# A speech joint network, forward and backward: GpSimd's sum of the tanh gradient over prompts, one instruction of 1024 columns or two of 512

## The chip, the core and the metric

The kernel runs on one core of a Trainium2 chip. The metric is the device time of one execution in microseconds (us); the time of a kernel is the median of its runs. The core has five engines with a queue of instructions each: TensorE (PE in the profile, its weight loads PEld), VectorE (DVE), ScalarE (ACT), GpSimd (POOL) and SyncE (SP), which here only issues DMAs. An engine works through its queue in order, and waits at an instruction until the semaphores it needs have been raised by others.

## The reference

All tensors are bfloat16. `x` has 2 x 16000 x 256 elements, the prompts `g` 2 x 8 x 256; `B`, `U`, `D` are 2, 8 and 256.

```python
h = gelu(conv(x, w1))[:, ::2]        # 3 taps, 256 -> 256, every second time step is kept
f = gelu(conv(h, w2))[:, ::2]        # the same again: 4000 steps per batch entry
fe = f @ w_f;  ge = g @ w_g
j  = tanh(fe[:, :, None, :] + ge[:, None, :, :])     # 4000 x 8 prompts x 256
out = j @ w_o
```

The kernel returns `out` and the gradients of all seven inputs for a given `grad_out` of the shape of `out`. For the gradient of `fe`, the gradient at the input of the tanh, `(grad_out @ w_o.T) * (1 - j*j)`, is summed over the eight prompts. That sum is what the change touches.

## The kernel before

The 4000 steps of each batch entry are cut into chunks of 512 (the last has 416), 16 chunks in all. Features lie on the 128 partitions, so that 256 features are two halves `kt` (0 and 1) side by side in a tile `[128, 2, 512]`.

The main loop (line 763) goes over the chunks `n`. For each it goes through four pairs of prompts. `joint_units` (603) is the main stream: for each prompt `u` of the pair `gj` (519) computes the tanh gradient, then comes the addition of `ngfe_acc` (537), and then the output product (line 624) and the gradient of `w_o` (line 673). `weave` (682) feeds two other things between the steps of this stream. The one is a list of units on TensorE: the two convolutions and the `w_f` product of chunk `n+1` (lines 244, 280, 303), and the backward pass of chunk `n-1` (lines 337, 367, 381 to 383, 407, 438, 479, 501). The other is `later`, a queue of single instructions of the two GELUs and their derivatives, of which `pump(2)` takes two at each step. They are all recorded at line 194 and run on VectorE, except for a sigmoid on ScalarE. So the order of each engine's queue follows from this weaving, and instructions of different parts stand close together.

The instructions that the prediction's steps touch:

- `gj`, line 532: for each half `mt`, VectorE reads the product of line 530 out of PSUM, multiplies it by `j*j - 1` (`JSQ`, squared by ScalarE at line 524) and writes one half of `NGZ`, the negated tanh gradient of this prompt. There are three buffers of `NGZ`. With the result VectorE also writes a sum over the columns, in a short instruction of its own after it (DVE_READ_ACCUMULATOR).
- `ngfe_acc`, line 551: GpSimd adds `NGZ` of prompts 0 and 1 into `ACCN` (float32), then one prompt after the other, and writes the sum with prompt 7 to `NGFE` (bfloat16): seven additions in a chunk, each over `[128, 1024]`. There is one buffer of `ACCN` and one of `NGFE`.
- Line 194 on VectorE: in the first part of a GELU `g_sq<-g_x` (a square, TENSOR_TENSOR), `g_sq<-g_sq` (a multiplication by a number, TENSOR_SCALAR), `g_s<-g_sq,g_x` (SCALAR_TENSOR_TENSOR), ScalarE's sigmoid, and `HT<-g_s,g_x`; in the second, `g_sq<-g_sq`, `g_x<-g_s`, `g_sq<-g_sq,g_x`, `g_sq<-g_sq,HT` and `G<-g_sq,g_s`. All their operands lie in SBUF.
- Lines 339, 370, 383, 323: VectorE's reads of the backward pass's products out of PSUM (`GF`, `GH`, `rows`, `ACC`).
- GpSimd's queue holds, besides the additions, the issues of the stores of `out` (line 653) and of the gradient of `x` (line 491), of the loads of `x` for the backward pass (line 180), and small copies of one or two columns at chunk borders (lines 235, 259, 263, 331, 343, 358, 374).

TensorE's products go through a ring of seven PSUM buffers (`psp`, line 96). A product can start when the engine that reads the product before it in the same buffer has done so.

Of the kernel before, what the change touches and what calls it, by code (L numbers as in the profile page):

```python
# [15 lines left out]
ALU = mybir.AluOpType  # L16
# [6 lines left out]
KT = 2  # L23
# [3 lines left out]
U = 8  # L27
# [4 lines left out]
def kernel(  # L32
# [22 lines left out]
    nc = tc.nc  # L55
# [7 lines left out]
    def geom(n):  # L63
        b, ci = chunks[n]
        c0 = ci * CW
        return b, ci, c0, min(CW, MQ - c0)
# [470 lines left out]
    def ngfe_acc(n, u):  # L537

        W = geom(n)[3]
        st = S[n]  # L540
        if u == 0:
            return
        if u == 1:
            st["ACCN"] = accp.tile([P, KT, CW], FP32, name="ACCN")
        acc = st["ACCN"][:, :, :W]
        in0 = st["NGZ", 0][:, :, :W] if u == 1 else acc
        out = acc
        if u == U - 1:
            st["NGFE"] = ngp.tile([P, KT, CW], BF16, name="NGFE")
            out = st["NGFE"][:, :, :W]  # L550
        nc.gpsimd.tensor_tensor(out=out, in0=in0, in1=st["NGZ", u][:, :, :W], op=ALU.add)  # L551

    def load_jr(n, up):

# [48 lines left out]
    def joint_units(n, up, ahead):  # L603
# [4 lines left out]
        for u in us:  # L608
            yield from gj(n, u)
            ngfe_acc(n, u)  # L610
            short_jt(n, u)
# [280 lines left out]
```

## Time and profile before

| | |
|---|---|
| median of 3 runs | 883.72 us (882.99 to 883.83) |
| the profiled execution's own time | 882.75 us |
| its span, from the first to the last instruction | 881.0 us |
| busy: PE, DVE, ACT, POOL | 833.0, 678.9, 639.0, 419.6 us |
| granted TensorE clock over the span | 0.993 |
| line 551 on POOL, by shape | 98 instructions of 1024 columns, 14 of 832; busy 247.8 us in all (162.7 + 30.2 + 30.2 + 17.7 + 3.5 + 3.5) |
| DVE instructions of line 532 | 256, 680 ns each for 512 columns |

The profile has a page with the busy time of the engines, the chain of work that ended last, and the costliest groups of instructions. The trace behind it can be asked for the order in time of each engine's instructions (the timeline), for who waited for whom, and for the chain in any stretch. A line of the timeline has the start in us, the duration in us, the engine, the line of the kernel, the operation, out<-in with the shape of the tile, how many were merged, and in brackets how long the engine was idle before it and whose instruction ended that.

The work between 120 and 800 us repeats chunk by chunk, every 52.7 us (the same addition starts at 553.47 and at 606.15 us), so one chunk can be read for most of them.

### The profile page before, as it was taken

Reading aid. Unit: us, or ns where it says so; the run is one execution under the profiler, and the core shown is the slowest. Engines: PE = TensorE matmul, PEld = TensorE weight load, DVE = VectorE, ACT = ScalarE, POOL = GpSimd, SP = SyncE. Lnnn points to the kernel's source line nnn. Section 1 sums busy time; section 2 is a strip of 40 time slices with the busy share of each in tenths; the row PEclk is TensorE's granted clock in tenths of the full one; section 3 lists DMA queues with packets and bytes.
Section 4 is the critical chain, followed back from the end, with each engine's and each line's share of the span. In section 5 each row is a group of like instructions: output and inputs, shape, how many; then the busy total and the mean of one; then the engine's idle time right before and its main releaser. Section 6 shows DMA issues by size and latency. Waiting matters only on the chain.

```text
span 881.0 us, 17824 instructions
## 1 busy us (share of the span) xinstructions
PE 833.0 (95%) x6574; PEld 600.6 (68%) x6648; DVE 678.9 (77%) x1296; ACT 639.0 (73%) x1016; POOL 419.6 (48%) x457
## 2 busy tenths in 40 slices
PE   7968999999999999998999999999999999999997
PEld 3545676767768577776756668676776757778875
DVE  5998959869596895959789596986959779596553
ACT  2767797686958769595786958768695876958534
POOL 1254544535535455553554544454554535554651
PEclk9998999999999999999999999999999999999999
DMA  9987999999999999999999999999999999997942
GB/s 207 183 182 164 191 229 233 219 210 231 239 227 229 239 179 258 196 227 214 183 197 201 250 219 224 246 230 250 198 227 225 222 237 194 229 209 175 225 136 94
DMA packets 382456, 185.67 MB, mean 211 GB/s; under 512 B 330160, under 2 KB 366280, under 8 KB 382368
## 3 DMA queue, kind: packets, MB, share of 16 engines
q1 hardware_dynamic: 362400, 114.35, 74.3%
q0 software_dynamic: 19968, 70.18, 26.9%
q8 instruction: 52, 0.85, 0.4%
q14 instruction: 36, 0.29, 0.1%
HBM read 54.43 MB, written 50.34 MB: 119 GB/s over the span
## 4 chain that ended last, share of the span: by engine, by line
PE 42%; DVE 29%; ACT 20%; issue 5%; DMA 2%; POOL 0%; ACTq 0%; POOLq 0%; DVEq 0%
DVE g_sq L194 10%; ACT JT L313 8%; PE GWO_ps L673 6%; PE ps L479 5%; PE ps L501 5%; PE ps L624 5%; DVE g_s L194 4%; PE ps L530 4%; PE ps L438 4%; PE ps L280 4%; PE pst L381 3%; DVE NGZ L532 3%; ACT GX L482 3%; DVE GH L370 3%; ACT JSQ L524 3%
## 5 line engine op out<-in xcount | busy, mean ns | idle before, releaser
L551 POOL TENSOR_TENSOR ACCN<-ACCN,NGZ 128x1024 f32<-128x1024 f32 (+1 forms) x80 | 180.3, 2254 | 174.5 <-DVE NGZ L532 173.3
L532 DVE SCALAR_TENSOR_TENSOR NGZ<-JSQ,ps 128x512 bf16<-128x512 bf16 (+1 forms) x256 | 164.2, 668 | 85.6 <-ACT GX L482 40.6
L524 ACT ACTIVATE JSQ<-JT 128x1024 bf16<-128x1024 bf16 (+1 forms) x128 | 135.3, 1059 | 76.2 <-DVE NGZ L532 76.2
L313 ACT ACTIVATE JT<-FE,GE 128x512 bf16<-128x512 f32 (+1 forms) x256 | 171.2, 738 | 0.1
L624 PE MATMUL ps<-WO,JT 128*128 128x256 bf16 x992 | 147.7, 273 | 5.7 <-DVE NGZ L532 4.9
L626 ACT CAST OUT<-ps 128x512 bf16<-128x512 f32 x248 | 143.4, 605 | 5.1 <-PE ps L624 4.7
L530 PE MATMUL ps<-GOT,WOT 128*128 128x512 bf16 (+1 forms) x472 | 134.2, 373 | 9.4 <-DVE GH L370 7.6
L673 PE MATMUL GWO_ps<-GO,JR 128*128 128x256 bf16 x992 | 139.0, 273 | 0.0
L194 ACT ACTIVATE g_s<-g_s 128x1024 bf16<-128x1024 bf16 (+2 forms) x49 | 49.3, 1005 | 98.0 <-DVE g_s L194 98.0
L624 PEld LDWEIGHTS <-JT 128*128 128x128 bf16 x992 | 94.6, 98 | 31.1 <-issue 9.5
L673 PEld LDWEIGHTS <-JR 128*128 128x128 bf16 x992 | 95.0, 98 | 23.8 <-issue 8.5
L323 DVE TENSOR_TENSOR ACC<-ACC,ps 128x512 f32<-128x512 f32 x90 | 59.2, 680 | 59.9 <-PE ps L501 55.3
L479 PE MATMUL ps<-W1T,GH 128*128 128x256 bf16 (+2 forms) x768 | 104.2, 273 | 0.4 <-ACT g_x L283 0.4
L501 PE MATMUL ps<-rows,X 128*128 128x256 bf16 (+2 forms) x768 | 92.3, 273 | 0.0
L244 PE MATMUL ps<-XC,W 128*128 128x512 bf16 (+1 forms) x370 | 88.6, 374 | 0.7 <-DMA XC<-in_x_dram 0.5
L482 ACT CAST GX<-ps 128x512 bf16<-128x512 f32 (+2 forms) x128 | 76.5, 598 | 14.1 <-PE ps L479 7.4
L479 PEld LDWEIGHTS <-GH 128*128 128x128 bf16 (+2 forms) x768 | 75.0, 99 | 15.9 <-issue 1.8
L501 PEld LDWEIGHTS <-X 128*128 128x128 bf16 (+2 forms) x768 | 74.6, 98 | 12.9 <-issue 1.3
L530 PEld LDWEIGHTS <-WOT 128*128 128x128 bf16 x512 | 49.0, 98 | 48.3 <-issue 9.5
L491 POOL DMA_DIRECT2D out_dram<-GX x64 | 35.7, 558 | 88.8 <-ACT GX L482 84.6
L653 POOL DMA_DIRECT2D out_dram<-OUT x64 | 49.4, 773 | 59.8 <-ACT OUT L626 54.7
L383 ACT COPY rows<-pst 128x1024 bf16<-128x1024 bf16 x64 | 64.2, 1013 | 10.7 <-PE pst L381 10.7
(135 smaller groups left out, 1324.0 us busy)
## 6 DMA issues: line engine op xcount, KB each, us to landing
GO<-in_grad_out_dram SPq DMA_DIRECT2D x56, 512.0 KB, 5.2
out_dram<-OUT POOLq DMA_DIRECT2D x56, 512.0 KB, 5.6
X<-in_x_dram POOLq DMA_DIRECT2D x58, 320.0 KB, 8.0
out_dram<-GX POOLq DMA_DIRECT2D x58, 256.0 KB, 3.8
JR<-JT SPq DMA_TRANSPOSE x240, 4.8
GO<-in_grad_out_dram SPq DMA_DIRECT2D x8, 384.0 KB, 4.0
out_dram<-OUT POOLq DMA_DIRECT2D x8, 384.0 KB, 4.9
GOT<-in_grad_out_dram SPq DMA_TRANSPOSE x128, 5.0
```

Source lines behind the costliest of these rows:

```text
L194: later.popleft()()
L313: nc.scalar.activation(out=JT[:, mt, :W], in_=S[n]["FE"][:, mt, :W], func=ACT.Tanh, bias=GE[:, b, mt, u:u + 1], scale=1.0)
L479: nc.tensor.matmul(ps[:Mx, cj * D:(cj + 1) * D], lhsT=GH[:, par, kt, j:j + Mx], rhs=W1T[:, i, kt, :], start=(k == 0), stop=(k == last))
L482: nc.scalar.copy(out=t[:Mx, 2 * cp:2 * cp + 2, :], in_=ps[:Mx, :])
L501: nc.tensor.matmul(ps[:, dt * D:(dt + 1) * D], lhsT=st["X5", o][:M, i + 2 * par, dt * P:(dt + 1) * P], rhs=t[:M, j + 2 * par:j + 2 * par + ...
L524: nc.scalar.activation(out=JSQ[:, :, :W], in_=JT[:, :, :W], func=ACT.Square)
L530: nc.tensor.matmul(ps[:, :W], lhsT=WOT[:, kt, mt * P:(mt + 1) * P], rhs=GOT[:, kt, :W], start=(kt == 0), stop=(kt == KT - 1))
L532: nc.vector.scalar_tensor_tensor(out=NGZ[:, mt, :W], in0=JSQ[:, mt, :W], scalar=1.0, in1=ps[:, :W], op0=ALU.subtract, op1=ALU.mult, accum_ ...
L551: nc.gpsimd.tensor_tensor(out=out, in0=in0, in1=st["NGZ", u][:, :, :W], op=ALU.add)
L624: nc.tensor.matmul(ps[:M, j * V:(j + 1) * V], lhsT=st["JT", u][:, kt, o:o + M], rhs=WO[:, kt, :], start=(kt == 0), stop=(kt == KT - 1))
L626: nc.scalar.copy(out=OUT[:M, k, :], in_=ps[:M, :])
L673: nc.tensor.matmul(GWO_ps[:, dt, :], lhsT=JR[:M, k, j, dt, :], rhs=GO[:M, k, j * V:(j + 1) * V], start=(n_gwo[0] == 0), stop=(n_gwo[0] == ...
```

## The change

The addition over `[128, 1024]` becomes two over `[128, 512]`, one for each half `kt`, first half first. In the built program the number of GpSimd's additions goes from 112 to 224, and each half waits for VectorE's instruction of line 532 that wrote this half alone. The queues of TensorE, VectorE, ScalarE and SyncE have the same instructions in the same order as before. In GpSimd's queue the two halves stand where the addition stood, except at eight places, where a copy of one or two columns (line 235, 331, 374, 573) or one store's issue (line 491) stands between two halves or has changed places with a first half.

```diff
-        acc = st["ACCN"][:, :, :W]
-        in0 = st["NGZ", 0][:, :, :W] if u == 1 else acc
-        out = acc
         if u == U - 1:
             st["NGFE"] = ngp.tile([P, KT, CW], BF16, name="NGFE")
-            out = st["NGFE"][:, :, :W]
-        nc.gpsimd.tensor_tensor(out=out, in0=in0, in1=st["NGZ", u][:, :, :W], op=ALU.add)
+        for kt in range(KT):
+            in0 = (st["NGZ", 0] if u == 1 else st["ACCN"])[:, kt, :W]
+            out = (st["NGFE"] if u == U - 1 else st["ACCN"])[:, kt, :W]
+            nc.gpsimd.tensor_tensor(out=out, in0=in0, in1=st["NGZ", u][:, kt, :W], op=ALU.add)
```

## Prediction

> **What bounds the kernel now.** I read the page first, then the chain of waits through one chunk, then the timelines of VectorE, GpSimd and TensorE there.
>
> ```profile
> PE 833.0 (95%) x6574; PEld 600.6 (68%) x6648; DVE 678.9 (77%) x1296; ACT 639.0 (73%) x1016; POOL 419.6 (48%) x457
> ...
> L551 POOL TENSOR_TENSOR ACCN<-ACCN,NGZ 128x1024 f32<-128x1024 f32 (+1 forms) x80 | 180.3, 2254 | 174.5 <-DVE NGZ L532 173.3
> ```
>
> GpSimd is busy for half of the span, and its additions mostly wait for VectorE. Nobody is listed as waiting for an addition. So GpSimd's own time is no term of the sum. What matters is what its additions do to VectorE. The timelines of one chunk, VectorE first:
>
> ```profile
> 554.31 1.83 DVE L194 TENSOR_TENSOR g_sq<-g_x 128x1024 bf16<-128x1024 bf16 x1 [0.40 <-ACT g_x L247]
> 556.17 0.43 DVE L194 TENSOR_SCALAR g_sq<-g_sq 128x1024 bf16<-128x1024 bf16 x1
> 556.63 1.23 DVE L194 SCALAR_TENSOR_TENSOR g_s<-g_sq,g_x 128x1024 bf16<-128x1024 bf16 x1
> ...
> 565.86 0.68 DVE L532 SCALAR_TENSOR_TENSOR NGZ<-JSQ,ps 128x512 bf16<-128x512 bf16 x1
> ...
> 566.47 0.68 DVE L532 SCALAR_TENSOR_TENSOR NGZ<-JSQ,ps 128x512 bf16<-128x512 bf16 x1
> ...
> 567.08 0.69 DVE L194 TENSOR_TENSOR g_sq<-g_sq,HT 128x1024 bf16<-128x1024 bf16 x1
> 567.68 0.68 DVE L370 TENSOR_TENSOR GH<-ps,G 128x512 bf16<-128x512 f32 x1
> ...
> 568.88 1.15 DVE L194 TENSOR_SCALAR g_sq<-g_sq 128x1024 bf16<-128x1024 bf16 x1
> ```
>
> ```profile
> 550.99 2.14 POOL L180 DMA_DIRECT2D X<-in_x_dram  x4
> 553.47 2.12 POOL L551 TENSOR_TENSOR ACCN<-NGZ 128x1024 f32<-128x1024 bf16 x1 [0.35 <-DVE NGZ L532]
> ...
> 567.31 2.44 POOL L551 TENSOR_TENSOR ACCN<-ACCN,NGZ 128x1024 f32<-128x1024 f32 x1 [5.84 <-DVE NGZ L532]
> 571.12 2.45 POOL L551 TENSOR_TENSOR ACCN<-ACCN,NGZ 128x1024 f32<-128x1024 f32 x1 [1.37 <-DVE NGZ L532]
> 573.52 0.65 POOL L235 COPY HT<-HT 128x2 bf16<-128x2 bf16 x1
> ```
>
> ```profile
> 566.61 0.60 PE L624 MATMUL ps<-WO,JT 128*128 128x256 bf16 x4 [0.19 <-DVE NGZ L532]
> ...
> 568.42 0.49 PE L381 MATMUL pst<-ident,HT 128*128 128x128 bf16 x6 [0.16 <-DVE GH L370]
> ```
>
> The square at 554.31 takes 1.83 us where the same form takes 0.68 undisturbed (560.78). The addition ends at 555.59, and the square 0.55 later. All 62 line-194 instructions that start well inside an addition behave so: a TENSOR_TENSOR of 1024 ends 0.55 us after the addition, a TENSOR_SCALAR 0.28 after it, so each stands still until the addition is over. In the other direction the addition at 567.31 takes 2.44 instead of 2.12, since `g_sq<-g_sq,HT` was already running. The 122 VectorE instructions that start inside an addition and read at most one operand from SBUF (NGZ, GH, rows, ACC) are not slowed: 0.68 as elsewhere. The 62 starts have 86.5 us of additions still ahead of them.
>
> Little of that is on the path:
>
> ```profile
> 554.31 1.84 DVE g_sq L194
> ...
> 566.47 0.69 DVE NGZ L532 x3
> 567.16 0.60 DVE g_sq L194
> 567.76 0.61 DVE GH L370
> 568.38 0.04 issue
> 568.42 0.61 PE pst L381 x8
> ```
>
> From 554.31 to 568.4 the chain runs through VectorE, and TensorE waits for it five times, last at 568.42. From there on TensorE has no wait on VectorE up to the next chunk, and the chain is TensorE's, then (588.5) ScalarE's. After 568.42 the next buffers that TensorE needs from VectorE are free 1.22, 1.40 and 2.44 us ahead. So of the four blocked instructions in a chunk (554.31, 568.88, 572.11, 582.45) only the first is on the path.
>
> **The change, step by step.** *A half's duration.* An addition of 1024 columns has a median of 2.12 us, one of 832 takes 1.76; that is 1.93 ns a column and 0.16 us fixed, so 1.14 us for 512 (bounds: 1.06, without any fixed part, to 1.30, with twice that). GpSimd's 112 more instructions cost 112 x 0.16 = 18 us, hidden by its 461 idle us except where told below.
>
> [...]
>
> *Who goes first between two halves.* At 573.57 an addition ends with a VectorE instruction waiting since 572.11 and the next GpSimd copy already issued (573.52): VectorE ends at 574.12, 0.55 later as always, and the tiny copy takes 0.65. So the one that waits longer goes first; I take this for the halves too.
>
> *Step A, the first blocked square (a gain).* The two NGZ of its prompt end at 551.68 and 553.31; the addition waits for the second. The first half need not, so it starts when GpSimd has issued the four loads (553.13), at 553.15, 0.32 earlier than now, and ends at 554.29. The square comes at 554.31, in a tie with the second half. If the half wins, the square ends at 556.00 instead of 556.14. If the square wins, it ends at 554.99, but the next instruction of line 194 (556.17 now) meets the second half, which ends at 556.05, and ends at 556.33 instead of 556.60. Either way `g_s` starts 0.14 to 0.27 earlier, not 1.1: the addition's time has only moved onto the instruction behind. I take 0.2. All VectorE work to 568 moves with it.
>
> *Step B, a new block (a loss).* The additions of prompt 2 start at 567.31, 0.15 after the second NGZ, and so miss `g_sq<-g_sq,HT`, which began at 567.08. The first NGZ ends at 566.54; GpSimd is idle then (5.84 us), so the first half runs from 566.70 to 567.84. `g_sq<-g_sq,HT` then ends at 567.84 + 0.55 = 568.39 instead of 567.76: 0.63 us lost (0.55 to 0.79 by the half's bounds). Behind it stands GH of 567.68, and TensorE's wait at 568.42 is for just this GH, with no slack (0.05 us). The second half goes from 568.29 to 569.43, clear of the TENSOR_SCALAR of 568.88, which now comes at 569.51 and is no longer blocked (0.7 us back, off the path). The next first half blocks an instruction at 569.9 for 0.9 us, which the 1.22 to 2.44 us of free buffers hide.
>
> Nine chunks have this pattern, with TensorE's wait for GH at 148.5, 201.2, 253.9, 307.2, 515.7, 568.4, 621.1, 673.8 and 726.5. B: 9 x 0.63 = +5.7 us. A: six of them alike, 6 x -0.2; one whose square comes 1.2 us into the addition, +0.1; one where the loads delay the addition now, -0.13; one where the addition could start 0.6 earlier (500.76, idle 0.59), -0.65. A: -1.9 us.
>
> *The first chunk (a gain).* From 34 to 69.4 us VectorE has no wait longer than 0.04 us and TensorE waits for it for 10 us in all (5.4 of these at 69.46 for FT). Five blocked instructions lie there (37.11, 43.53, 47.62, 60.95, 66.46; 8.2 us together). Replayed by the rules above, with the halves put in where their NGZ ends, VectorE's lead grows -0.5, -0.8, -1.7, falls to -1.3 where a first half meets `G<-g_sq,g_s` at 57.8, and goes -1.9, -1.4, -2.4 to -1.9 at FT. I take -1.5, since ScalarE and TensorE must deliver earlier too; bounds 0 and -2.4.
>
> *The other chunks.* The second: a first half at 92.8 blocks a TENSOR_SCALAR for 1.0 us, and the NGZ behind it is needed by TensorE 0.35 later: +0.5. Those of 345 and 764: -0.1 each; of 396: -0.3; of 448: +0.1, its step B hidden by 0.79 us. After 800 no GELU is left to block. Together +0.1.
>
> *What GpSimd's queue holds.* Stores of GX and OUT, loads and small copies stand behind the additions. The last two additions of a chunk (591.75 to 593.88, 594.41 to 596.54) would end 0.4 and 0.1 us earlier, so stores are issued no later; ScalarE waits for such a store only 0.2 us (339.09). The eight changed places in the queue move small copies by one half's time: nothing. NGFE is ready at 845 and first read after 850: nothing. No stall is simply gone: what is late after A is the second half, and after B the GH.
>
> Sum: 5.7 - 1.9 - 1.5 + 0.1 = +2.4 us on the profiled 882.75: 885.15. The median of the runs is 0.97 above it, so I give 883.72 + 2.4 = **886.1 us**, 0.27% slower.
>
> **Rivals.** *Faster, B does not come.* If the first half starts later than 567.08 (a longer way from NGZ to GpSimd than the 0.15 us of 567.31), only A, the first chunk and small terms stay: -1.9 - 1.5 - 0.4 = -3.8, 879.9 us. For: 0.38 us decide it. Against: 0.15 us is the same in nearly all additions.
>
> The Trainium skill (SBUF, "Who interferes with whom") says that a GpSimd instruction and a VectorE instruction with two SBUF inputs lock each other out for the whole instruction; the 62 rows show it. Read alone it speaks for the change, as half the hold is half the block: half of 86.5 is 43 us of VectorE's time. The rows keep from this only what the chain holds.
>
> *Much slower, GpSimd keeps going.* If the second half goes before a waiting VectorE instruction, step B costs 1.14 more: 9 x 1.77 = 15.9, less some 1.5 for A and the first chunk, 898 us. For: at 764.64 an addition follows a load's issue at once, and a square that waits since 764.26 comes after it. Against: the copies at 573.52 and in its like.
>
> *Nothing.* A and the first chunk's gain pay for B (first chunk at -2.4, B at 0.55 and not in all nine), or TensorE makes up the delay: within 1 us of 883.7.
>
> **Chances.** Forecast 0.50, B absent 0.24, GpSimd keeps going 0.09, nothing 0.17. A measurement of this kernel can tell about 0.2% (1.8 us) from no change. The forecast's own range is 884.5 to 889; 0.07 of its 0.50 falls within 0.2%. Of "B absent" 0.22 is faster by more, 0.02 within. So faster 0.22, same 0.07 + 0.02 + 0.17 = 0.26, slower 0.43 + 0.09 = 0.52. The range goes from 879.5 (B absent) to 891 (B at 0.79, and the second chunk's pattern in two or three more); it leaves out "GpSimd keeps going".
>
> **What would show it.** Right: halves of 1.1 to 1.2 us; `g_sq<-g_sq,HT` after NGZ of prompt 2 at 1.3 instead of 0.69, TensorE's wait for GH 0.6 longer; the first square near 0.7 or 1.7, with the next TENSOR_SCALAR at 1.3 or 0.43; FT of the first chunk 1 to 2 us earlier. Wrong: `g_sq<-g_sq,HT` still at 0.69 (faster), or at 2.4 (much slower).

## The result and the profile after

| | before | after |
|---|---|---|
| median of 10 runs each, on one chip | 883.19 us (880.86 to 885.65) | 886.93 us (884.41 to 890.95) |
| ratio | | 1.0045, 95% interval 1.0026 to 1.0065 |
| the profiled execution's own time | 882.75 us | 885.5 us |
| its span | 881.0 us | 883.7 us |
| busy on DVE and POOL | 678.9, 419.6 us | 661.1, 436.6 us |

The kernel became 0.45% slower. The page of the profile after, busy time and the additions (line 550 now, since the lines after 551 have moved up by one):

```profile
PE 837.6 (95%) x6648; PEld 600.4 (68%) x6648; DVE 661.1 (75%) x1296; ACT 643.8 (73%) x1016; POOL 436.6 (49%) x569
...
L550 POOL TENSOR_TENSOR ACCN<-ACCN,NGZ 128x512 f32<-128x512 f32 (+1 forms) x160 | 192.2, 1218 | 142.3 <-DVE NGZ L532 142.2
```

GpSimd is busy 17.0 us longer for its 112 more additions, and VectorE 17.8 us *shorter*. By these sums alone the change would look good. The timelines of the same chunk tell why it is not. VectorE after:

```profile
554.07 1.66 DVE L194 TENSOR_TENSOR g_sq<-g_x 128x1024 bf16<-128x1024 bf16 x1 [0.37 <-ACT g_x L247]
...
566.66 1.32 DVE L194 TENSOR_TENSOR g_sq<-g_sq,HT 128x1024 bf16<-128x1024 bf16 x1
567.91 0.68 DVE L370 TENSOR_TENSOR GH<-ps,G 128x512 bf16<-128x512 f32 x1
...
569.11 0.42 DVE L194 TENSOR_SCALAR g_sq<-g_sq 128x1024 bf16<-128x1024 bf16 x1
569.45 1.38 DVE L194 TENSOR_SCALAR g_x<-g_s 128x1024 bf16<-128x1024 bf16 x1
570.75 0.68 DVE L532 SCALAR_TENSOR_TENSOR NGZ<-JSQ,ps 128x512 bf16<-128x512 bf16 x1
```

GpSimd after (an entry with x2 is both halves, one behind the other):

```profile
552.90 2.27 POOL L550 TENSOR_TENSOR ACCN<-NGZ 128x512 f32<-128x512 bf16 x2
...
566.29 2.72 POOL L550 TENSOR_TENSOR ACCN<-ACCN,NGZ 128x512 f32<-128x512 f32 x2 [5.24 <-DVE NGZ L532]
569.34 1.21 POOL L550 TENSOR_TENSOR ACCN<-ACCN,NGZ 128x512 f32<-128x512 f32 x1 [0.33 <-DVE NGZ L532]
```

TensorE after:

```profile
568.64 0.50 PE L381 MATMUL pst<-ident,HT 128*128 128x128 bf16 x6 [0.80 <-DVE GH L370]
...
572.59 1.34 PE L438 MATMUL ps<-rows 128*128 128x256 bf16 x8
```

and the eight products of line 438 before:

```profile
572.37 1.11 PE L438 MATMUL ps<-rows 128*128 128x256 bf16 x8
```

Three things are to be seen. The first square takes 1.66 instead of 1.83 us. `g_sq<-g_sq,HT` takes 1.32 instead of 0.69, since prompt 2's first half started at 566.29, 0.37 ahead of it; TensorE's wait for GH at 568.64 is 0.80 instead of 0.16. And prompt 3's first half (569.34) holds up `g_x<-g_s` (1.38 instead of 0.41), and the NGZ after it starts at 570.75, where the chunk's work is otherwise 0.22 us later than before (570.29 there, 0.46 in all). The eight matrix products of line 438 took 1.11 us before and take 1.34 now: there is a wait inside them, which the next section but one follows.

A table by chunk makes the sum. The start of the first `GF` (line 339) of a chunk is the mark; what an interval between two marks grew or shrank, in the profiled executions:

| stretch (times of before) | change in us |
|---|---|
| start to 80.65 (first chunk) | -2.6 |
| 80.65 to 133.29 (second) | -0.3 |
| nine chunks with TensorE's wait for GH | +0.99, 0.68, 0.68, 1.00, 0.45, 0.68, 0.66, 0.68, 0.68: +6.5 |
| the four others up to 812 | -0.01, -1.10, -0.01, +0.28: -0.8 |
| 812 to the end | 0.0 |
| sum | +2.8 |

### The profile page after: what moved, and what is told of

Read it like the earlier page. It is cut to its first block, busy times and chain, and to the rows that moved or that the text cites. A ratio compares the mean times of both kernels' runs of the same rounds, so it can differ in the third digit from the quotient of the medians.

```text
span 883.7 us, 18103 instructions
## 1 busy us (share of the span) xinstructions
PE 837.6 (95%) x6648; PEld 600.4 (68%) x6648; DVE 661.1 (75%) x1296; ACT 643.8 (73%) x1016; POOL 436.6 (49%) x569
## 4 chain that ended last, share of the span: by engine, by line
PE 44%; DVE 27%; ACT 23%; issue 5%; DMA 1%; POOL 0%; ACTq 0%; DVEq 0%; POOLq 0%
DVE g_sq L194 9%; ACT JT L313 8%; PE ps L479 6%; PE ps L501 6%; PE GWO_ps L672 6%; PE ps L530 5%; PE ps L623 5%; PE ps L280 4%; PE ps L438 4%; DVE NGZ L532 4%; DVE g_s L194 4%; ACT JSQ L524 4%; PE pst L381 3%; DVE GH L370 3%; ACT GX L482 2%
## 5 line engine op out<-in xcount | busy, mean ns | idle before, releaser
L550 POOL TENSOR_TENSOR ACCN<-ACCN,NGZ 128x512 f32<-128x512 f32 (+1 forms) x160 | 192.2, 1218 | 142.3 <-DVE NGZ L532 142.2
L532 DVE SCALAR_TENSOR_TENSOR NGZ<-JSQ,ps 128x512 bf16<-128x512 bf16 (+1 forms) x256 | 166.1, 670 | 99.2 <-PE ps L530 47.3
L530 PE MATMUL ps<-GOT,WOT 128*128 128x512 bf16 (+1 forms) x512 | 138.3, 374 | 7.7 <-DVE GH L370 7.5
L244 PE MATMUL ps<-XC,W 128*128 128x512 bf16 (+1 forms) x384 | 91.2, 375 | 1.0 <-DMA XC<-in_x_dram 1.0
```

The costliest lines, as they stand in the source:

```text
L530: nc.tensor.matmul(ps[:, :W], lhsT=WOT[:, kt, mt * P:(mt + 1) * P], rhs=GOT[:, kt, :W], start=(kt == 0), stop=(kt == KT - 1))
L532: nc.vector.scalar_tensor_tensor(out=NGZ[:, mt, :W], in0=JSQ[:, mt, :W], scalar=1.0, in1=ps[:, :W], op0=ALU.subtract, op1=ALU.mult, accum_ ...
```

## Experiments

Theory 1 is the prediction's, with what the profile after adds: a half matters only where it starts or ends otherwise than the whole addition did, relative to a line-194 instruction on the path. So splitting prompt 1 and the first chunk gains, splitting prompts 2 and 3 loses, and the loss reaches TensorE by named waits (GH, rows). The rival, theory 2: the loss comes with 112 more GpSimd instructions and is spread over all of them, wherever they stand.

A condition chooses where the addition is split; all else is as before. The four queues other than GpSimd's hold the same instructions in the same order in every experiment:

```diff
+        for ks in ((slice(0, 1), slice(1, 2)) if COND else (slice(0, 2),)):
+            in0 = (st["NGZ", 0] if u == 1 else st["ACCN"])[:, ks, :W]
+            out = (st["NGFE"] if u == U - 1 else st["ACCN"])[:, ks, :W]
+            nc.gpsimd.tensor_tensor(out=out, in0=in0, in1=st["NGZ", u][:, ks, :W], op=ALU.add)
```

**u2_only.** COND is `n > 0 and u == 2`.

> Only the addition of prompt 2 is split, in all chunks but the first. Theory 1 (a half that starts early blocks one VectorE instruction on the path): TensorE's last wait for GH in nine chunks goes from 0.16 to 0.80 us as after the change, with some 0.6 us in the second chunk; +6 us, ratio 1.007, more than the whole change. The wait for rows from ScalarE (0.13 us after the change) is not there, since that comes from prompt 3. Theory 2 (each added GpSimd instruction costs its fixed time): 15 of 112 additions are split, so 15/112 of the change's +2.7 us, +0.4 us, ratio 1.0004.

Measured: 888.88 us, ratio 1.0053 (1.0037 to 1.0069). Six regular chunks grew by 0.55 to 0.57 us each (the three other chunks of this kind by 0.65 to 1.28), and the timeline of TensorE has step B's wait in full:

```profile
572.31 0.49 PE L381 MATMUL pst<-ident,HT 128*128 128x128 bf16 x6 [0.80 <-DVE GH L370]
```

The kernel lost somewhat less than the 6 us and the ratio of 1.007 that were expected, but one prompt of seven, split, costs as much as all seven. Theory 2 falls here, and step B is shown by itself.

**u3_only.** COND is `n > 0 and u == 3`.

> Only the addition of prompt 3 is split, in all chunks but the first. Theory 1 with a leak through ScalarE: prompt 2's whole addition ends at about 569.75 in the chunk read before, prompt 3's first half comes right behind the TENSOR_SCALAR that waited and holds g_x<-g_s until about 571.1 (1 us later), so the second NGZ, ScalarE's square and ScalarE's copy of rows come up to 1 us later, and TensorE waits for rows in nine chunks: +0.2 to +1.0 us each, +2 to +9 us, ratio 1.002 to 1.010. The rival, that only the PSUM buffers matter (1.2 to 2.4 us free there): no change, ratio 1.000. Theory 2 (fixed cost per instruction): +0.4 us.

Measured: 894.06 us, ratio 1.0110 (1.0090 to 1.0129), the slowest of all. The prediction held that prompt 3's half costs nothing. TensorE's and VectorE's timelines:

```profile
579.02 0.49 PE L381 MATMUL pst<-ident,HT 128*128 128x128 bf16 x6 [0.16 <-DVE GH L370]
...
584.66 0.39 PE L438 MATMUL ps<-rows 128*128 128x256 bf16 x2 [0.87 <-ACT rows L383]
```

```profile
579.49 1.16 DVE L194 TENSOR_SCALAR g_sq<-g_sq 128x1024 bf16<-128x1024 bf16 x1
580.57 1.38 DVE L194 TENSOR_SCALAR g_x<-g_s 128x1024 bf16<-128x1024 bf16 x1
```

The wait for GH is back at 0.16, and there is a new one of 0.87 us: TensorE waits for ScalarE's copy of `rows`. Here prompt 2's whole addition blocks the first of the two TENSOR_SCALARs (as before the change) and prompt 3's half the second, so NGZ is later than in the change, where only the second is blocked. Six regular chunks grew by 0.95 to 1.00 us each; nine such chunks make some 9 us, near the 9.4 between the medians. The profiled execution (897.94, the slowest) grew by more in three chunks: two hold waits for transfers (3.1 us for a store of GX, 1.8 us for a load of JR), and the third a gap of 2.0 us for which the profile names no cause.

**u1_and_first.** COND is `n == 0 or u == 1`.

> All seven additions of the first chunk and prompt 1's in all others are split; the rest stay whole. Theory 1: the gains of the change without its losses: -2.4 us from the first chunk, 0.17 us in nine chunks and 0.5 us in one, -4 to -5 us, ratio 0.995. Theory 2: 22 of 112 additions are split, +0.5 us, ratio 1.0006.

Measured: 880.86 us, ratio 0.9961 (0.9946 to 0.9975). The first chunk's interval shrank by 2.3 us (counted from ScalarE's first square, at 32.61 in before, ahead of any addition), the regular ones by 0.14 to 0.20 each: step A and the first chunk, by themselves.

**u2_u3_whole.** The change with prompts 2 and 3 left whole after the first chunk: COND is `not (n > 0 and u in (2, 3))`.

> The change, with the additions of prompts 2 and 3 whole again in all chunks but the first. Theory 1: all losses are undone, the halves of prompts 4 to 7 meet nothing on the path: as with prompt 1 and the first chunk alone, -3 to -5 us, ratio 0.996. Theory 2: 82 of 112 additions are still split, +2 us, ratio 1.002.

Measured: 880.21 us, ratio 0.9951 (0.9927 to 0.9975). Regular chunks again -0.15 to -0.18. So prompts 4 to 7 may be split or not, and two places in the chunk carry the whole loss.

**second_first.** The change, with the halves in the other order: `for kt in (1, 0):`.

> As many halves as after the change, but the second half of the features is added first, so that no half starts before both NGZ are written. Theory 1: step B's block is gone (GH's wait back to 0.16 us), the first chunk keeps some 2 us of its gain, prompt 1's square 0.1 us a chunk; a TENSOR_SCALAR before prompt 3's second NGZ may lose 0.2 us a chunk. Together -4 to 0 us, likeliest -2, ratio 0.998. Theory 2: as after the change, +2.7 us, ratio 1.003 to 1.0045.

Measured: 887.48 us, ratio 1.0032 (1.0018 to 1.0045): a miss. The order in the source decided little. In the built program only prompt 1's halves were turned round, in 15 chunks of 16; for the other prompts the half whose NGZ is ready first came first again. So step B stayed (GH wait of 0.80, a chunk +0.73). The turned prompt 1 still answers one question, who goes first between two halves. VectorE there, with the halves running one behind the other from 554.12 to 556.83:

```profile
554.96 0.85 DVE L194 TENSOR_TENSOR g_sq<-g_x 128x1024 bf16<-128x1024 bf16 x1 [0.40 <-ACT g_x L247]
555.85 1.26 DVE L194 TENSOR_SCALAR g_sq<-g_sq 128x1024 bf16<-128x1024 bf16 x1
```

The square waits for the first half, runs (0.85 us), and the TENSOR_SCALAR waits for the second. VectorE's waiting instruction goes in between, though GpSimd's second half has nothing to wait for.

**column_halves.** The halves are cut across both `kt`, so each half waits for both NGZ and no half can start earlier than the whole addition did:

```diff
+        for cs in (slice(0, W // 2), slice(W // 2, W)):
+            in0 = (st["NGZ", 0] if u == 1 else st["ACCN"])[:, :, cs]
...
```

> The additions are split into two halves of the columns instead of the features, so that as many pieces of the same size are there, but none can start before both NGZ are written. Theory 1 (early halves block the path): GH's wait stays at 0.16 us in the nine chunks; prompt 1's square gains 0.13 us a chunk; the second half of prompt 2 ends 0.2 to 0.3 us later than the whole addition, which comes back through NGZ, ScalarE's square and rows as a wait of some 0.2 us a chunk; the first chunk gains 2 us. Together -3 to +1 us, likeliest -1, ratio 0.999. Theory 2 (each added instruction costs its fixed time): as after the change, +2.7 us or more, ratio 1.003 to 1.0045.

Measured: 880.71 us, ratio 0.9953 (0.9932 to 0.9975), better than expected. As many GpSimd instructions as the change, as short, and no loss: theory 2 falls a second time. VectorE:

```profile
550.66 0.86 DVE L194 TENSOR_TENSOR g_sq<-g_x 128x1024 bf16<-128x1024 bf16 x1 [0.39 <-ACT g_x L247]
551.56 1.26 DVE L194 TENSOR_SCALAR g_sq<-g_sq 128x1024 bf16<-128x1024 bf16 x1
...
563.30 0.69 DVE L194 TENSOR_TENSOR g_sq<-g_sq,HT 128x1024 bf16<-128x1024 bf16 x1
```

The square is short, but what it saves is taken by the instruction behind it, and `g_sq<-g_sq,HT` is untouched. From 500 us to 763 the chunks are as long as before to within 0.02 us, so shorter holds by themselves gain nothing there. The gain is at the start: -2.3 up to ScalarE's first square, -1.7 from there to the first mark, -1.0 in the second chunk. The first of these lies ahead of any addition's effect: all kernels run the same instructions up to there, and the profiled executions reach that point between 2.3 us earlier and 0.8 us later than before's. So -2.7 is the additions' part. The chunk at 396 is 1.1 shorter, as in the change; four others are 0.3 to 1.3 longer in this execution, for a cause that stays open.

**loads_later_split.** If an early start is the gain, then it should be made earlier still where it helps. In before the four loads of `x` stand ahead of prompt 1's addition in GpSimd's queue (550.99 to 553.13) and hold the first half back. COND as in u1_and_first, and the loads are issued after that addition:

```diff
-            for (o, M) in blocks(window(n - 1)[1] - window(n - 1)[0]):
-                load_x5(n - 1, o, M)
...
+                if back and up == 0:
+                    for (o, M) in blocks(window(n - 1)[1] - window(n - 1)[0]):
+                        load_x5(n - 1, o, M)
```

> As in the run with prompt 1 and the first chunk split, and GpSimd issues the four loads of x for the backward pass after prompt 1's addition instead of ahead of it. The first half can then start at about 551.85 in the chunk read before and the second at 553.47, which ends at 554.6; the square that comes at 554.31 ends at 555.2 instead of 556.14, and nothing blocks the instruction behind it. Theory 1: 0.7 to 1.0 us in some 13 chunks, as the chain runs through this square and TensorE's waits behind it (2 us a chunk) give room, and 2.4 us in the first chunk: -10 to -16 us, ratio 0.982 to 0.989. The rival, that another engine is next at once, or that the loads now come late for the gradient of w1: -3 to -5 us as without the move.

Measured: 871.55 us, ratio 0.9851 (0.9817 to 0.9884), the fastest of all, and faster than both kernels. GpSimd and VectorE in one of its chunks:

```profile
652.26 1.15 POOL L550 TENSOR_TENSOR ACCN<-NGZ 128x512 f32<-128x512 bf16 x1 [0.85 <-DVE NGZ L532]
653.81 1.15 POOL L550 TENSOR_TENSOR ACCN<-NGZ 128x512 f32<-128x512 bf16 x1 [0.41 <-DVE NGZ L532]
```

```profile
654.74 0.78 DVE L194 TENSOR_TENSOR g_sq<-g_x 128x1024 bf16<-128x1024 bf16 x1 [0.40 <-ACT g_x L247]
```

The first half now runs while VectorE computes the second NGZ, both are over at 654.96, and the square takes 0.78 us. Chunks undisturbed by transfers shrank by 0.54 to 0.68 us. (The profiled execution, 877.15 us, is its slowest; ScalarE waits there 4.5 us for stores of GX.)

**loads_later_whole.** The loads later, no addition split.

> The kernel before, whole additions, with the four loads of x issued after prompt 1's addition. The addition still waits for the second NGZ (553.32) and starts at 553.47 as before, so the move alone gives nothing but in the four chunks where the loads delayed it by 0.1 to 0.2 us: -1 to 0 us, ratio 0.999 to 1.000. If the loads themselves (and not the halves) made the difference, -10 us as with the split.

Measured: 880.75 us, ratio 0.9954 (0.9934 to 0.9973), where no change was expected. The profiled execution couldn't tell why: it took 884.9 us, with 5.4 us of ScalarE's waits for stores of GX. So a second execution of the same kernel was profiled, **loads_later_whole_b**.

> The same kernel as loads_later_whole, for a second profiled execution: the first took 884.9 us where the median was 880.75, and held 5.4 us of ScalarE's waits for stores of GX. If these waits are the difference, an execution near 880.5 has less than 1 us of them, with the chunk's period at 52.7 us, and what it gains on the kernel before are TensorE's waits for GF in the chunks at 297, 349 and 769 us (0.77, 0.67 and 1.16 us before, gone or shorter here). If the gain lies elsewhere, the period itself is shorter than 52.7 us.

This execution took 880.78 us and held 0.6 us of such waits. The regular chunks are as long as before to 0.05 us. Three intervals shrank, by 0.70, 0.46 and 0.96 us, together 2.1: those that end at the marks 344, 396 and 812, and in each of them TensorE's wait for GF went or shrank (0.77 to none, 0.67 to 0.20, 1.16 to 0.20). The last, before and here, GpSimd and then TensorE:

```profile
764.64 2.14 POOL L551 TENSOR_TENSOR ACCN<-NGZ 128x1024 f32<-128x1024 bf16 x1
```

```profile
762.70 2.12 POOL L550 TENSOR_TENSOR ACCN<-NGZ 128x1024 f32<-128x1024 bf16 x1 [1.21 <-DVE NGZ L532]
```

```profile
769.36 0.38 PE L367 MATMUL ps<-GF,W2T 128*128 128x512 bf16 x1 [1.16 <-DVE GF L339]
```

```profile
767.39 0.38 PE L367 MATMUL ps<-GF,W2T 128*128 128x512 bf16 x1 [0.20 <-DVE GF L339]
```

In that chunk the loads did hold the addition, and the addition the square (2.98 us, 2.02 now). In the regular chunks the addition waited for NGZ anyway. That is 2.1 us of the 3.8 between the two medians of that comparison (880.78 and 884.62); the executions of before that were timed there took 883 to 887 us, the profiled one 882.75, and what the former have more was not seen.

**loads_later_change.** The whole change on top of the later loads (COND always true).

> The change in full (two halves, each waiting for its own NGZ, at every prompt), with the four loads of x (line 180) issued after prompt 1's addition. Theory 1 (each first half that starts before a line-194 instruction costs the path, wherever the loads stand): the loads later free the first square (0.55 to 0.69 us less per chunk, as in loads_later_split), but prompts 2 and 3 still cost 0.63 + 0.23 us per chunk in nine or ten chunks; so +0.2 per chunk and -2.5 in the first chunk, within 2 us of the kernel before: 0.997 to 1.001, and some 11 us slower than loads_later_split. TensorE's wait for GH 0.8 us in each chunk, its wait for rows 0.13. Theory 2 (the loads between the additions were what made the halves costly): as loads_later_split, 0.982 to 0.989, with waits for GH of 0.16.

Measured: 878.63 us, ratio 0.9939 (0.9920 to 0.9958): outside what theory 1 gave (0.997 to 1.001), and much slower than loads_later_split, so the expectation's theory 2 falls. The mechanism of theory 1 held: regular chunks grew by 0.17 to 0.20 us, TensorE waits 0.80 us for GH in nine of them. What was left out of the sum are the intervals that end at 344, 396 and 812, which shrank by 0.52, 0.41 and 0.91, much as in loads_later_whole_b, and the one that ends at 446, which shrank by 1.75 (1.10 in the change without the move, nothing in loads_later_whole_b). Next to loads_later_split the halves of prompts 2 to 7 cost 7 us.

**loads_later_cols.** Columns as in column_halves, loads later.

> The additions split by columns (each half waits for both NGZ), with the loads of x after prompt 1's addition. Theory 1 (an early start of the first half ahead of the blocked instruction is the only gain, and the only loss): the first addition still starts 0.35 us after the second NGZ, loads or not, so the square is blocked in any case and a chunk is as before, within 0.05 us; what is gained is the start (2 to 4 us, as in column_halves) and the waits for GF in the chunks at 297, 349 and 769 us (2.6 us): 0.990 to 0.995. Theory 2 (the shorter hold is a gain in itself once the loads are gone): near loads_later_split, 0.982 to 0.988.

Measured: 878.63 us, ratio 0.9937 (0.9916 to 0.9957), as theory 1 had it. Regular chunks as before to 0.01 us: an addition that waits for both NGZ gains nothing from having the loads out of its way.

## Why the prediction was right, and where it was not

It gave 886.1 us, +2.4 on the profiled execution; the median is 886.93, the profiled execution +2.75. Direction and size came out, by these steps:

- *A half's duration*: 1.15 to 1.17 us in the middle of the halves of 512 columns against 1.14; GpSimd +17.0 us against 18. (The working is a little off: 2.12 and 1.76 us, as written there, make 1.88 ns a column, 0.20 us fixed and 1.16 us for a half.)
- *Who goes first between two halves*: VectorE's waiting instruction, at all nine places of step B, and most plainly in second_first and column_halves. (In after, 83 instructions of line 194 start well inside a half and stand at least until it ends, where 62 did inside whole additions.) So the rival "GpSimd keeps going" is out where it was priced. It is not out everywhere. In after, the second half went ahead of the waiting square in five chunks, with squares at 78.66, 291.88, 345.49, 500.45 and 766.74; in each the first half had run right behind GpSimd's issues of loads. In two others of that kind (396.56, 449.76) VectorE came in between. One of the five, VectorE and then both halves:

```profile
291.88 2.65 DVE L194 TENSOR_TENSOR g_sq<-g_x 128x1024 bf16<-128x1024 bf16 x1 [0.39 <-ACT g_x L247]
```

```profile
291.70 2.27 POOL L550 TENSOR_TENSOR ACCN<-NGZ 128x512 f32<-128x512 bf16 x2
```

The square ends at 294.53, 0.56 us after the second half. It is blocked as long as by the whole addition (2.52 us, at 292.45 of before), and this chunk grew by 1.00 us instead of 0.68.
- *Step A*: 0.17 to 0.18 us at 554.07, the tie won by the half; u1_and_first shows 0.14 to 0.20 a chunk. Taken: 0.2. Right.
- *Step B*: instruction for instruction. First half at 566.29 to 567.44 (0.15 us behind its NGZ), `g_sq<-g_sq,HT` 1.32, TensorE's wait 0.64 longer (0.63 taken), at each of the nine places. u2_only shows it alone. "B absent" is out.
- *The step that failed* is the last sentence of step B: "The next first half blocks an instruction at 569.9 for 0.9 us, which the 1.22 to 2.44 us of free buffers hide." The block came (569.45, 1.38 us). It was looked for only where VectorE hands a PSUM buffer to TensorE, and there it was indeed hidden. But the NGZ behind it also frees its `JSQ` buffer, of which there are two, and ScalarE's next square waits for that. ScalarE before, and after:

```profile
571.07 1.06 ACT L524 ACTIVATE JSQ<-JT 128x1024 bf16<-128x1024 bf16 x1
572.04 0.99 ACT L383 COPY rows<-pst 128x1024 bf16<-128x1024 bf16 x1
```

```profile
571.53 1.06 ACT L524 ACTIVATE JSQ<-JT 128x1024 bf16<-128x1024 bf16 x1 [0.84 <-DVE NGZ L532]
572.49 0.99 ACT L383 COPY rows<-pst 128x1024 bf16<-128x1024 bf16 x1
```

Before, ScalarE came to this square without waiting; now it waits 0.84 us for NGZ, and the copy of `rows` queued behind it is later by as much as the square, 0.45 us, 0.22 of which the rest of the chunk is late anyway. TensorE needs these rows at once: 0.23 us more in a chunk, inside line 438. u3_only shows the way by itself, at 0.87 us. So a regular chunk grew by 0.64 + 0.23 - 0.18, that is 0.69 (0.66 to 0.68 measured), not 0.43. Over nine chunks this is +2.1 us that the sum did not have.
- *The first chunk* was mis-sized in the other direction: -1.5 taken, the replay by rules gave -1.9, and it measured -2.6 in after (-2.8 from ScalarE's first square), of which TensorE's waits between 46 and 70 us give 2.4 (10.2 us before, 7.8 after), and -2.3 in u1_and_first. The discount "since ScalarE and TensorE must deliver earlier too" was not needed.
- *The other chunks*: the second got the wait foreseen for NGZ (0.51 us at 92.28), but two of its waits vanished (0.35 us for `g_x`, 0.27 for FT), so -0.3 instead of +0.5. The one at 396 gained 1.1 instead of 0.3, since a wait of 0.77 us for rows fell away. The four together are -0.8 against -0.4.

So the nine chunks have +6.5 against +3.8, and the rest -3.7 against -1.4. The total is near because two errors of some 2.5 us have opposite signs: that part was luck. What was not: A and B were both right to 0.03 us a chunk, with B the larger. But with the other chunks as they were measured, A and B alone would have left some +0.7 us, which the medians could hardly tell from nothing. That the kernel is clearly slower is owed to the path through ScalarE as well.

The Trainium skill (SBUF — State Buffer, "Who interferes with whom") lets a GpSimd instruction and a VectorE instruction with two SBUF inputs exclude each other for a whole instruction; the 83 blocked rows agree. But half the hold was not half the block: the time still ahead of blocked instructions fell from 86.5 us only to 63.7, since there were 83 instead of 62, and of the ten more `g_sq<-g_sq,HT` among them (23 instead of 13) nine are on the path.

## What to carry to other kernels

Cutting an instruction that holds up another engine does two things, and they are to be priced apart: the hold gets shorter, and its first part may start earlier, where it meets other instructions. Here the shorter hold was worth nothing in a regular chunk (column_halves), and the earlier start decided everything: a loss where it ran into the path's next instruction, a gain of 0.6 us a chunk where it was given room to finish ahead of it (loads_later_split). When a delay is called hidden, follow every resource that the delayed instruction frees, through the other engines' queues, not only the one that the bottleneck engine takes from it.

## What the runs showed of the hardware

- At the hand-over between two GpSimd instructions that follow at once, a VectorE instruction of line 194 that has been waiting comes in between (square 0.85 us, next instruction 1.26, in second_first). Not always: where the first of the two runs right behind GpSimd's issues of loads, the second went first in five of seven places in after (2.65 us for the square at 291.88). At 764.26 of before, too, a square that had started 0.38 us ahead of an addition ended after it, 2.98 us long, and that addition followed such issues at once. Yet at 655.55 of loads_later_split a TENSOR_SCALAR runs in 0.43 us while loads are issued. What decides who goes first behind the loads is open.
- ScalarE's wait for stores of GX differs from one execution to another of the same kernel: 5.4 us in one of loads_later_whole, 0.6 in the other, and the times 884.9 and 880.8 us go with it. One profiled execution is not the median; the comparison of chunks that have no such wait is.
